# A fused attention, MLP and Strassen-gated MLP kernel: where the last layer's output products stand around the seventh product of a block of tokens

## The chip, the cores and the metric

The kernel runs on 1 core of a Trainium2 chip. The metric is the device time of one execution in microseconds (us); shorter is better. Engines are named as the profile names them: PE is TensorE's matmuls, PEld its weight loads, DVE is VectorE, ACT is ScalarE, POOL is GpSimd, SP is the queue that issues most of the DMAs.

## The reference

Three stages run one after the other on 3072 tokens. The change touches the last alone.

```
def reference(...):
    attn_out = _attn_ref(q, k, v, mem_k, mem_v)      # chunked attention, 4 x 8 heads x 768 x 64
    x = attn_out.transpose(0, 2, 1, 3).reshape(3072, 512)
    h = x @ w_in                                     # 512 -> 2048
    x = np.maximum(0.01 * h, h) @ w_out              # 2048 -> 512
    return ((x @ w_a) * (x @ w_b)) @ w2_out          # 512 -> 1536, gated, -> 512
```

All numbers are float32. The kernel splits each operand into a high and a low part (`hi`, `lo`), and takes three matmuls where a product of float32 numbers is wanted: low by high, high by low, high by high.

## The kernel before, in words

The last layer is computed for three blocks of 1024 tokens each (`sb` = 0, 1, 2; `NS` is 3), two halves of 512 tokens per block. Its 1536 hidden columns are taken in six pairs of 256 (`p` = 0..5; `k` counts all 18 pairs). Every 2 x 2 block product is done by Strassen's scheme in Winograd's form: seven products instead of eight.

`layer3(k, m)` is a generator that makes the seven products of one pair for `w_a` (`m` = 0) or `w_b` (`m` = 1). `stage(k, m, pos)` runs it on by one product, `pos` 0 to 6. A product is 6 matmuls 128x512 into one PSUM bank; the banks are called A, B, C and D, and A and C take more than one product each. At `pos` 4 VectorE adds the copied bank A (`u3`) to bank C (`done(1, 1, ...)`, L897); `pos` 5 is a product into D; `pos` 6, the seventh product, goes on accumulating into C and can do so only when that addition has read C. With `m` = 1 each sum is multiplied by what `m` = 0 left (`ga`) and is then split by `parts`: a cast on ACT (L126) and a subtraction on DVE (L127) make one `st` tile. `st` 0 comes after `pos` 1, `st` 2 after `pos` 4, `st` 1 after `pos` 5. After the seventh product `done(0, 1, ...)` adds the copied `u2` to C, and a chain of additions and subtractions on DVE makes four more: `st` 3, 4, 6 and 5, in this order.

`product4(sb, g, j, i)` is an output product: two pairs (a group `g`, three per block), row block `j` of 128 tokens (0 to 3), Strassen index `i` (0 to 6). It is 6 matmuls 128x256; the first three take the `st` tile of the even pair, the last three that of the odd pair, which is the newer one. Index 0, 4, 5 goes to a bank `oa`, the others to `oc`; there are two banks of each, so rows 2 and 3 take over those of rows 0 and 1. DVE adds banks to `acc` in SBUF (L982), and after the last group a row is stored.

Groups 0 and 1 of a block have their output products spread over the products of the next pair: `PLAN` says which batch of `BATCH` follows which `pos`. The last group of a block has no next pair of its own. There (`end`), PE is held to the order of the code (`pe.on`; the other engines are not, and a scheduler puts their instructions into an order when the program is built). For blocks 0 and 1 the batches are mixed with the first products of the next block: these are the two **changes of tokens**. For block 2 the list `LAST` is run: **the end**. At a change the operands of the next block, `xc_make(sb + 1, i)`, are made too: subtractions of 128x1024 on DVE (L754, `xs`), a cast on ACT (`ch`) and a subtraction on DVE (`cl`).

The lines 44 and 47 are those of `InOrder`, the helper that holds an engine to the order of the code: a matmul after `pe.on` has one of them, whatever it computes; the tiles tell it apart.

Of the kernel before, what the change touches and what calls it, by code (L numbers as in the profile page):

```python
# [53 lines left out]
def kernel(  # L54
# [680 lines left out]
    def xs_load(sb):  # L735
        for h, tag in enumerate(("xh", "xh" if sb else "xl")):
            t = xp.tile([P, KC, TB], F32, tag=tag, name="xs")
            nc.sync.dma_start(out=t, in_=x2d[2 * sb + h])
            xs[sb, h] = t
# [8 lines left out]
    def xc_make(sb, i):  # L748
        (b11, b21), (b12, b22) = [
            (xs[sb, h][:, 0:HC, :], xs[sb, h][:, HC:KC, :]) for h in range(2)  # L750
        ]

        def sub(out, x, y):
            nc.vector.tensor_tensor(out=out, in0=x, in1=y, op=ALU.subtract)  # L754

        if i == 0:
            xc_parts(sb, 0, b11)
            sub(b11, b12, b11)
        elif i == 1:
            xc_parts(sb, 1, b21)  # L760
        elif i == 4:
            xc_parts(sb, 3, b11)
            sub(b11, b22, b11)
            xc_parts(sb, 4, b11)
        elif i == 5:
            sub(b12, b22, b12)
            xc_parts(sb, 5, b12)
        elif i == 2:
            sub(b21, b21, b11)
            xc_parts(sb, 2, b21)  # L770
        elif i == 6:
            xc_parts(sb, 6, b22)
# [20 lines left out]
    for bi, f, parts in items[LEAD:]:  # L793
# [20 lines left out]
        if not first:  # L814
            wo_load((bi - 1) * NF1 + f + 4)

            i = (bi - 1) * NF1 + f
# [39 lines left out]
    def wt_load(sb, g, r):  # L857
        t = wq.tile([P, 2, 2, 256], F32R, tag="wt", name="wt", bufs=7)
        nc.sync.dma_start(out=t.bitcast(F32), in_=wtd[g][:, r])
        wts[sb, g, WT[r]] = t  # L860
# [92 lines left out]
    def product4(sb, g, j, i):  # L953
# [55 lines left out]
                store(1, low, both)  # L1009

    BATCH = (
# [6 lines left out]
    )  # L1018
    LAST = [(j, i) for j in range(4) for i in (0, 2)] + [(j, 3) for j in range(4)]
    LAST += [(j, i) for j in range(4) for i in (4, 6, 1, 5)]  # L1020

    def batch(sb, g, *ns):
        for n in ns:
            for j, i in BATCH[n]:
                product4(sb, g, j, i)
# [4 lines left out]
    def stage(k, m, pos):  # L1030
        if made.get((k, m), 0) == pos:
            next(stages[k, m])
            made[k, m] = pos + 1

    PLAN = (
        {2: (0, 1), 4: (2,), 5: (3,)},
        {0: (4,), 1: (5,)},
    )

    for k, (sb, p) in enumerate(pairs):  # L1040
        if p == 2 and sb + 1 < NS:
            xs_load(sb + 1)
        g, odd = divmod(p, 2)
        for m in range(2):
            end = p == NP - 1 and m == 1
            for pos in range(6):
                stage(k, m, pos)
                if pos == 0 and (k or m):
                    stage(*((k, 0) if m else (k - 1, 1)), 6)
                if not odd and p:  # L1050
                    batch(sb, g - 1, *PLAN[m].get(pos, ()))
                if odd and not m:
                    for r in (pos, 6)[:1 + (pos == 5)]:
                        wt_load(sb, g, r)
                if end and sb + 1 < NS and pos < 2:
                    xc_make(sb + 1, pos)
            if end:
                pe.on, pe.last = True, None
                stage(k, m, 6)
                if sb + 1 == NS:  # L1060
                    for j, i in LAST:
                        product4(sb, g, j, i)
                    break
                batch(sb, g, 0)
                stage(k + 1, 0, 0)
                batch(sb, g, 1)
                stage(k + 1, 0, 1)
                batch(sb, g, 2)
                xc_make(sb + 1, 4)
                batch(sb, g, 3)  # L1070
                xc_make(sb + 1, 5)
                batch(sb, g, 4)
                xc_make(sb + 1, 2)
                batch(sb, g, 5)
                xc_make(sb + 1, 6)
                for pos in range(2, 6):
                    stage(k + 1, 0, pos)
                pe.on = False
# [66 lines left out]
```

## Time and profile before

| | before |
|---|---|
| time, median of 3 runs | 1146.77 us (1145.92 to 1147.29) |
| the profiled execution's own time | 1145.8 us |
| its span, first to last instruction | 1144.0 us |
| PE busy | 1122.0 us, 98% |
| DVE busy | 803.2 us, 70% |
| ACT busy | 476.8 us, 42% |
| granted TensorE clock, mean | 0.996 of full speed |

Busy time is an average over three very different stages; what DVE does around the changed places is read from those places. Matmuls overlap, so that the distance from one start to the next tells what a matmul costs, and its own duration does not.

### The profile page before, as it was taken

What the parts mean: (1) busy time and instruction counts of PE and PEld (TensorE: products, weight loads), DVE (VectorE), ACT (ScalarE), POOL (GpSimd) and SP (SyncE); (2) the same over time, 40 slices, a digit from 0 to 9 for tenths busy, and PEclk for the clock granted to TensorE, in tenths of its full rate; (3) what the DMA queues carried; (4) which work ended last, traced back from release to release, by engine and by line L of the source; (5) the groups of instructions that cost most, each with busy time, mean ns of one, the idle gap of its engine ahead of it and who ended that gap; (6) DMA issues with size and microseconds to landing.
All of it is one profiled execution on the core that took longest, in us unless ns stands there. A gap on an engine that the chain in (4) does not pass through costs nothing.

```text
span 1144.0 us, 18008 instructions
## 1 busy us (share of the span) xinstructions
PE 1122.0 (98%) x6992; PEld 958.6 (84%) x6992; DVE 803.2 (70%) x1485; ACT 476.8 (42%) x806; POOL 6.3 (1%) x16
## 2 busy tenths in 40 slices
PE   6899999999999999999999999999999999999998
PEld 6678888888888888888888898989898979898987
DVE  6899499879978964645112838597747689656767
ACT  5787565555555544325223424152333142333221
POOL 2000000000000000000000000000000000000000
PEclk9999999999999999999999999999999999999999
DMA  9977899899999984326346765657856566747451
GB/s 349 328 267 283 313 327 312 319 349 336 308 345 331 333 312 166 124 93 225 106 147 224 254 211 176 203 165 259 277 172 204 173 207 212 231 155 227 148 184 74
DMA packets 89380, 269.68 MB, mean 236 GB/s; under 512 B 9552, under 2 KB 10960, under 8 KB 88528
## 3 DMA queue, kind: packets, MB, share of 16 engines
q1 hardware_dynamic: 88992, 268.21, 69.0%
q8 instruction: 55, 0.90, 0.3%
q10 hardware_dynamic: 304, 0.33, 0.1%
q14 instruction: 29, 0.24, 0.1%
HBM read 214.50 MB, written 54.00 MB: 235 GB/s over the span
## 4 chain that ended last, share of the span: by engine, by line
PE 86%; DVE 5%; DMA 2%; ACT 1%; issue 0%; SPq 0%; DVEq 0%; ACTq 0%
PE h L413 7%; PE a L533 7%; PE a L537 7%; PE a L536 7%; PE h L415 6%; PE h L414 6%; PE A L868 4%; PE A L869 4%; PE A L870 4%; PE C L868 3%; PE C L869 3%; PE C L870 3%; PE oc L972 2%; PE oc L971 2%; PE oc L970 2%; PE oc L47 2%
## 5 line engine op out<-in xcount | busy, mean ns | idle before, releaser
L413 PE MATMUL h<-xh,w 128*128 128x512 f32 (+1 forms) x384 | 151.8, 395 | 3.1 <-ACT w L47 3.1
L533 PE MATMUL a<-gh,w 128*128 128x512 f32 (+1 forms) x392 | 150.8, 385 | 0.9 <-DVE w L183 0.7
L536 PE MATMUL a<-gl,w 128*128 128x512 f32 (+1 forms) x392 | 150.5, 384 | 0.0
L537 PE MATMUL a<-gh,w 128*128 128x512 f32 (+1 forms) x392 | 150.4, 384 | 0.0
L415 PE MATMUL h<-xh,w 128*128 128x512 f32 (+1 forms) x384 | 149.2, 388 | 0.0
L414 PE MATMUL h<-xl,w 128*128 128x512 f32 (+1 forms) x384 | 149.0, 388 | 0.0
L431 DVE TENSOR_TENSOR gl<-g,gh 128x512 fp32r<-128x512 f32 (+1 forms) x96 | 65.2, 679 | 95.0 <-ACT gh L430 94.3
L126 ACT CAST st<-gb 128x512 fp32r<-128x512 f32 x126 | 76.5, 621 | 107.5 <-DVE gb L897 107.2
L515 ACT ACTIVATE g<-h 128x512 f32<-128x512 f32 (+1 forms) x96 | 56.3, 587 | 110.6 <-PE h L415 110.1
L127 DVE TENSOR_TENSOR st<-gb,st 128x512 fp32r<-128x512 f32 x126 | 85.3, 689 | 12.9 <-ACT st L126 10.7
L893 ACT COPY u<-A 128x512 f32<-128x512 f32 x72 | 42.2, 586 | 124.5 <-PE A L870 114.6
L413 PEld LDWEIGHTS h<-xh,w 128*128 128x128 f32 x384 | 72.4, 188 | 18.6 <-ACT w L47 3.2
L533 PEld LDWEIGHTS a<-gh,w 128*128 128x128 f32 x392 | 73.8, 188 | 16.3 <-DVE w L183 1.1
L536 PEld LDWEIGHTS a<-gl,w 128*128 128x128 f32 x392 | 73.8, 188 | 14.5
L537 PEld LDWEIGHTS a<-gh,w 128*128 128x128 f32 x392 | 73.7, 188 | 14.5
L415 PEld LDWEIGHTS h<-xh,w 128*128 128x128 f32 x384 | 72.4, 189 | 14.8
L414 PEld LDWEIGHTS h<-xl,w 128*128 128x128 f32 x384 | 72.5, 189 | 14.1 <-DVE xl L47 0.4
L346 DVE STREAM_TRANSPOSE pt<-p 32x128 f32<-32x128 f32 x256 | 77.4, 303 | 4.3
L868 PE MATMUL A<-ch,wab 128*128 128x512 f32 x204 | 79.5, 390 | 0.0
L869 PE MATMUL A<-cl,wab 128*128 128x512 f32 x204 | 79.5, 390 | 0.0
L870 PE MATMUL A<-ch,wab 128*128 128x512 f32 x204 | 79.4, 389 | 0.0
L897 DVE TENSOR_TENSOR ga<-u,C 128x512 f32<-128x512 f32 x36 | 24.7, 686 | 55.8 <-PE C L870 36.2
(162 smaller groups left out, 2331.6 us busy)
## 6 DMA issues: line engine op xcount, KB each, us to landing
wab<-wab SPq DMA_DIRECT2D x126, 512.0 KB, 4.3
w<-wod SPq DMA_DIRECT2D x80, 512.0 KB, 4.7
raw<-w SPq DMA_DIRECT2D x68, 512.0 KB, 6.7
wt<-wtd SPq DMA_DIRECT2D x63, 512.0 KB, 4.8
k<-kl SPq DMA_DIRECT2D x48, 256.0 KB, 4.8
v<-vl SPq DMA_DIRECT2D x48, 256.0 KB, 5.0
wab<-pwb SPq DMA_DIRECT2D x12, 768.0 KB, 6.3
wod<-w SPq DMA_DIRECT2D x16, 512.0 KB, 6.2
```

What stands on the lines that cost most here:

```text
L126: act.copy(hi, z)
L127: eng.tensor_tensor(out=lo, in0=z, in1=hi.bitcast(F32), op=ALU.subtract)
L346: dve.transpose(out=pt[o0:o0 + 32, :, 2 * cpar + hpar, hpx, :], in_=p[i0:i0 + 32, hpx::2, 32 * b:32 * b + 32],)
L413: pe.matmul(ps, w[1], x[0], start=first, stop=False)
L414: pe.matmul(ps, w[0], x[1], start=False, stop=False)
L415: pe.matmul(ps, w[0], x[0], start=False, stop=last)
L533: pe.matmul(ps, slot[:, 1, c], gh[:, t], start=f == 0 and o == 0, stop=False, **kw)
L536: pe.matmul(ps, slot[:, 0, c], gl[:, t], start=False, stop=False, **kw)
L537: pe.matmul(ps, slot[:, 0, c], gh[:, t], start=False, stop=f == NF1 - 1 or (o == HALF and f == LEAD - 1), **kw)
L868: pe.matmul(ps, w[:, 1, c], hi[:, kc], start=first and kc == 0, stop=False, **kw)
L869: pe.matmul(ps, w[:, 0, c], lo[:, kc], start=False, stop=False, **kw)
L870: pe.matmul(ps, w[:, 0, c], hi[:, kc], start=False, stop=kc == HC - 1, **kw)
```

## The change

At a change of tokens the first batch, rows 0 and 1 of index 0 and 2, is split in two: index 0 of both rows comes ahead of the seventh product, index 2 behind it. The products of index 3 come behind the second product of the next block instead of between its first and second. `PLAN` is renumbered for the longer list, so in the six groups inside the blocks the order of the same four products becomes 0, 0, 2, 2 instead of 0, 2, 0, 2. At the end the same two products of index 0 come ahead of the seventh product, and the products of index 3 of rows 2 and 3 move from the common start into rows 0 and 1.

```
     BATCH = (
-        [(0, 0), (0, 2), (1, 0), (1, 2)],
+        [(0, 0), (1, 0)],
+        [(0, 2), (1, 2)],
         [(0, 3), (1, 3)],
         [(0, 4), (0, 6), (0, 1), (1, 4), (1, 6), (1, 1)],
...
-    LAST = [(j, i) for j in range(4) for i in (0, 2)] + [(j, 3) for j in range(4)]
-    LAST += [(j, i) for j in range(4) for i in (4, 6, 1, 5)]
+    LAST = [(2, 0), (3, 0)] + [(j, 2) for j in range(4)] + [(0, 3), (1, 3)]
+    for j in range(4):
+        LAST += [(j, i) for i in (4, 6, 1)] + [(j + 2, 3)] * (j < 2) + [(j, 5)]
...
     PLAN = (
-        {2: (0, 1), 4: (2,), 5: (3,)},
-        {0: (4,), 1: (5,)},
+        {2: (0, 1, 2), 4: (3,), 5: (4,)},
+        {0: (5,), 1: (6,)},
     )
...
                 pe.on, pe.last = True, None
+                batch(sb, g, 0)
                 stage(k, m, 6)
...
-                batch(sb, g, 0)
+                batch(sb, g, 1)
                 stage(k + 1, 0, 0)
-                batch(sb, g, 1)
                 stage(k + 1, 0, 1)
-                batch(sb, g, 2)
+                batch(sb, g, 2, 3)
                 xc_make(sb + 1, 4)
-                batch(sb, g, 3)
+                batch(sb, g, 4)
                 xc_make(sb + 1, 5)
-                batch(sb, g, 4)
+                batch(sb, g, 5)
                 xc_make(sb + 1, 2)
-                batch(sb, g, 5)
+                batch(sb, g, 6)
                 xc_make(sb + 1, 6)
```

On PE, at the first change of tokens, the order differs as follows (`-` before, `+` changed). A row is an instruction: tile written, tiles read, shape. `C_7512` is the bank of the seventh product, `oa` the banks of index 0, `st_7495` the `st` 0 of the newer pair.

```order
-L44 MATMUL C_7512<-ch6_5926,wab_7430 128x512
+L44 MATMUL oa_7548<-wt_7398,st_7299 128x256
+L47 MATMUL oa_7548<-wt_7398,st_7299 128x256 x2
+L47 MATMUL oa_7548<-wt_7398,st_7495 128x256 x3
+L47 MATMUL oa_7556<-wt_7398,st_7299 128x256 x3
+L47 MATMUL oa_7556<-wt_7398,st_7495 128x256 x3
+L47 MATMUL C_7512<-ch6_5926,wab_7430 128x512
```

Two output products, 12 matmuls, now stand between the sixth product and the seventh.

On DVE, at the same place, the kernel before has this order from the addition that reads the finished C to the subtraction that makes `st` 3 (`st_7560`), and on to `st` 4 (`st_7565`).

```order
L897 TENSOR_TENSOR gb_7556<-u2_7510,C_7512 128x512
L127 TENSOR_TENSOR st_7532<-gb_7529,st_7532 128x512
L897 TENSOR_TENSOR gb_7556<-gb_7556,ga_7478 128x512
L127 TENSOR_TENSOR st_7545<-gb_7542,st_7545 128x512
L897 TENSOR_TENSOR gb_7529<-gb_7556,gb_7529 128x512
L982 TENSOR_TENSOR acc_6527<-acc_6527,oa_7575 128x256
L897 TENSOR_TENSOR gb_7556<-gb_7492,gb_7556 128x512
L127 TENSOR_TENSOR st_7560<-gb_7529,st_7560 128x512
L897 TENSOR_TENSOR gb_7492<-gb_7529,gb_7492 128x512
L982 TENSOR_TENSOR acc_6527<-acc_6527,oa_7590 128x256
L897 TENSOR_TENSOR gb_7542<-gb_7542,gb_7492 128x512
L127 TENSOR_TENSOR st_7565<-gb_7492,st_7565 128x512
```

The changed kernel has this order on DVE there (`st_7532` is `st` 2, `st_7576` is `st` 3, `st_7581` is `st` 4).

```order
L982 TENSOR_TENSOR acc_6527<-acc_6527,oa_7548 128x256
L127 TENSOR_TENSOR st_7532<-gb_7529,st_7532 128x512
L127 TENSOR_TENSOR st_7545<-gb_7542,st_7545 128x512
L982 TENSOR_TENSOR acc_6527<-acc_6527,oa_7556 128x256
L897 TENSOR_TENSOR gb_7572<-u2_7510,C_7512 128x512
L754 TENSOR_TENSOR xs_6461<-xs_6463,xs_6461 128x1024
L897 TENSOR_TENSOR gb_7572<-gb_7572,ga_7478 128x512
L754 TENSOR_TENSOR xs_6463<-xs_6463 128x1024
L897 TENSOR_TENSOR gb_7529<-gb_7572,gb_7529 128x512
L897 TENSOR_TENSOR ga_7623<-a1_7612,B_7614 128x512
L897 TENSOR_TENSOR gb_7572<-gb_7492,gb_7572 128x512
L127 TENSOR_TENSOR st_7576<-gb_7529,st_7576 128x512
```

The additions of index 0 and the tiles `st` 2 and `st` 1 moved ahead of the addition that reads C; two subtractions for the next block (L754) and the next block's `ga_7623` moved in between that addition and `st` 3. Behind the last row come, one after the other, `gb_7492`, the addition of index 3 of row 0, `gb_7542`, and `st` 4. The second change of tokens has the same orders with other numbers.

On PE, at the end, the changed kernel has this order behind the products of index 2 (`st_10861`, `st_10866`, `st_10870` are `st` 3, 4, 6 of the newest pair).

```order
L47 MATMUL oc_10892<-wt_10736,st_10861 128x256 x3
L47 MATMUL oc_10899<-wt_10736,st_10687 128x256 x3
L47 MATMUL oc_10899<-wt_10736,st_10861 128x256 x3
L47 MATMUL oa_10835<-wt_10748,st_10692 128x256 x3
L47 MATMUL oa_10835<-wt_10748,st_10866 128x256 x3
L47 MATMUL oc_10892<-wt_10725,st_10696 128x256 x3
L47 MATMUL oc_10892<-wt_10725,st_10870 128x256 x3
```

One product of index 3 (row 1) stands between that of row 0 and the first of index 4, where before three did.

## Rows read from the trace of the kernel before

**Rows 1.** The page, its first line.

```profile
span 1144.0 us, 18008 instructions
```

**Rows 2.** Who PE waited for, whole span: us in total, times, longest.

```profile
PE s L44 <- DMA k<-kl: 5.4, 1, 5.4
...
PE C L44 <- DVE gb L897: 1.8, 2, 0.9
...
PE oa L47 <- DVE acc L982: 0.9, 1, 0.9
...
PE oc L47 <- DVE st L127: 0.6, 2, 0.3
```

**Rows 3.** Timeline of PE, first change: start, us, instructions, [idle before <-releaser].

```profile
762.36 0.39 PE L870 MATMUL D<-ch,wab 128*128 128x512 f32 x1
763.67 0.50 PE L44 MATMUL C<-ch,wab 128*128 128x512 f32 x1 [0.92 <-DVE gb L897]
764.01 0.40 PE L47 MATMUL C<-cl,wab 128*128 128x512 f32 x1
...
766.73 0.62 PE L47 MATMUL oc<-wt,st 128*128 128x256 f32 x3 [0.31 <-DVE st L127]
...
770.01 1.60 PE L47 MATMUL oc<-wt,st 128*128 128x256 f32 x12
771.45 0.40 PE L47 MATMUL B<-ch,wab 128*128 128x512 f32 x1
...
777.14 1.60 PE L47 MATMUL oa<-wt,st 128*128 128x256 f32 x12
...
780.02 2.01 PE L47 MATMUL oa<-wt,st 128*128 128x256 f32 x12
```

**Rows 4.** Busy time in the first change of tokens: PE, PEld, DVE, ACT, POOL, clock, DMA.

```profile
756.00:791.00 35.00, 33.62 (x225) 30.60 (x224) 34.54 (x51) 12.27 (x18) 0.00 (x0) 1.00 0.56 174
```

**Rows 5.** Timeline of DVE, first change.

```profile
762.33 0.69 DVE L127 TENSOR_TENSOR st<-gb,st 128x512 fp32r<-128x512 f32 x1
762.93 0.68 DVE L897 TENSOR_TENSOR gb<-u,C 128x512 f32<-128x512 f32 x1
...
764.13 1.29 DVE L897 TENSOR_TENSOR gb<-gb,ga 128x512 f32<-128x512 f32 x2
...
768.39 0.41 DVE L982 TENSOR_TENSOR acc<-acc,oa 128x256 f32<-128x256 f32 x1
768.73 0.68 DVE L897 TENSOR_TENSOR gb<-gb 128x512 f32<-128x512 f32 x1
769.33 0.68 DVE L127 TENSOR_TENSOR st<-gb,st 128x512 fp32r<-128x512 f32 x1
...
776.84 1.22 DVE L754 TENSOR_TENSOR xs<-xs 128x1024 f32<-128x1024 f32 x1
777.98 0.68 DVE L982 TENSOR_TENSOR acc<-acc,oc 128x512 f32<-128x512 f32 x1
```

**Rows 6.** Timeline of PEld, first change: the weight load of the seventh product.

```profile
763.67 0.19 PEld L44 LDWEIGHTS C<-ch,wab 128*128 128x128 f32 x1 [1.35 <-DVE gb L897]
```

**Rows 7.** Timeline of PE, the end.

```profile
1116.73 0.39 PE L870 MATMUL D<-ch,wab 128*128 128x512 f32 x1
1117.21 0.50 PE L44 MATMUL C<-ch,wab 128*128 128x512 f32 x1
...
1130.58 1.70 PE L47 MATMUL oa<-wt,st 128*128 128x256 f32 x12 [0.93 <-DVE acc L982]
...
1139.32 0.88 PE L47 MATMUL oa<-wt,st 128*128 128x256 f32 x6
```

**Rows 8.** Busy time and clock, microseconds 23 and 26, columns as in rows 4.

```profile
23.00:24.00 1.00, 1.00 (x10) 0.77 (x9) 0.97 (x2) 0.69 (x5) 0.00 (x0) 0.50 1.05 426
...
26.00:27.00 1.00, 1.00 (x9) 1.00 (x8) 0.97 (x3) 0.61 (x2) 0.00 (x0) 0.82 1.03 410
```

**Rows 9.** Timeline of PE ahead of those microseconds.

```profile
21.18 0.38 PE L47 MATMUL h<-xh,w 128*128 128x256 f32 x1 [1.34 <-ACT xh L47]
```

## The prediction

> **What bounds the kernel now.** The list of what PE waited for comes first [rows 2]: apart from waits at the very start (the longest is 5.4 us, for the first keys), the waits that the change can touch are four lines long. The seventh product waits for the addition that reads C twice, 0.9 us each; an index 2 product waits for its `st` tile twice, 0.3 us; one product at the end waits 0.9 us for a bank. No DMA stands in these places, so the moved stores and loads on the SP queue are costed at nothing: what covers them is that PE's late waits are all for DVE.
>
> The timeline of PE shows what such a wait costs [rows 3]. 512-column matmuls start 0.23 us apart, so D's last slot ends at 762.59; C starts at 763.67, which is 1.08 us lost, and its second matmul comes 0.34 us later instead of 0.23: 0.11 us more for starting again. Twelve 256-column matmuls take 771.45 - 770.01 = 1.44 us, 0.12 each and 0.72 a product. The index 2 wait shows 0.31 us idle.
>
> The busy time of the same stretch is the view that decides [rows 4]: in 35 us around the first change DVE is busy 34.5 us, PE 33.6. DVE is as full there as PE. The kernel's 70% for DVE hides this. So the question is not whether the C wait goes, but in which order DVE does the same work.
>
> **The change, part by part.** Inside the blocks four products change their order in six groups; the `st` tiles are old there, and DVE's order stays the same, so 0. If a tile were late after all it would show as a wait of the kind in [rows 2]; there is none outside the listed places.
>
> *The first change of tokens*, walked with these steps: on DVE [rows 5] a 512-wide instruction 0.60 us after the one before (762.33, 762.93), 256-wide 0.34 (768.39, 768.73), 1024-wide 1.14 (776.84, 777.98), results 0.08 us later; handing over takes 0.06 (an `st` 0 that starts at 762.33 and lasts 0.69 is free to PE at 763.08).
>
> PE: index 0 of rows 0 and 1 starts at 762.59, waits 0.11 us for `st` 0 at 763.08 in the middle, ends at 764.25. C follows with no wait, since its reader ends at 763.61: the 1.08 us are gone. C ends at 765.6; the second half of index 2 would start at 765.98.
>
> DVE: the two multiplications at 764.13 and 764.73, then by the new order the addition of index 0 at 765.33, `st` 2 at 765.66, done 766.34. PE waits until 766.40, 0.43 us, as before. Index 2 ends at 767.58, the next block's A at 768.95, B at 770.31; the first half of index 3 at 770.67. Now it needs `st` 3.
>
> DVE's list up to `st` 3: `st` 1 at 766.26, an addition at 766.86, the reader of C at 767.19, the first subtraction for the next block at 767.79, a multiplication at 768.93, the second subtraction at 769.53, the sum at 770.67, `ga` of the next block at 771.27, a difference at 771.87, `st` 3 at 772.47 to 773.15. Before, the same tile was made at 769.33 [rows 5] and PE had reached index 3 at 770.01 [rows 3], with 0.3 us to spare for its second half. Now PE waits from 770.67 to 773.21: **2.54 us**, and three instructions of 1.14, 1.14 and 0.60 us are the reason. ACT adds nothing: its casts for the next block end before the `st` 3 cast is wanted at DVE.
>
> Then the rest of the chain is late too, since nothing stands between index 3 and index 4 any more, where before the 1.4 us of B stood. DVE: difference 773.07, index 3's addition at 773.83 (it needs the product), difference 774.43, `st` 4 at 775.03 to 775.71. PE has done (1, 3) at 774.4 and half of (0, 4) at 774.75: a wait of 1.02 us. `st` 6 follows an addition at 775.63 and is free at 776.97; PE waits 0.38 us. With 0.1 us for each new start, four more products bring PE to index 5 at 780.3. Before that was 777.14 [rows 3]: +3.17 us. One hidden wait goes (the twelve matmuls at 780.02 last 2.01 us instead of 1.60, so 0.41), and one like it comes, 0.31 us, for the addition of index 3 of row 2. **+3.1 us a change**, +6.2 for two, since the waits at the second change are the same to 0.1 us [rows 2]. Bounds: 2.5 us, the one large wait without its followers minus the removed C wait and so +1.3, if DVE catches up at once; 4.1, if every hand-over costs 0.1 more. All of it lies on the path, for PE has no slack behind it.
>
> *The end* is walked with the same steps, from D's last slot at 1116.96 [rows 7]. The start of C loses 0.25 + 0.11 us now, and the bank wait 1.08 + 0.1; both go: -1.5. The seventh product ends at 1119.77, 1.07 us later than before (1.44 of index 0 less 0.36), and only two rather than four products of index 3 stand ahead of index 4. The addition at `pos` 4 starts at 1116.47 (its end released C at 1117.21), and by its list DVE reads the finished C at 1120.3 and makes `st` 3 seven instructions later: free at 1124.7 where PE wants it at 1124.45. Five more make `st` 4 free at 1127.3 against 1126.2, and `st` 6 is 0.38 us late. With new starts that is +1.9. Sum: +0.3 us, PE ending at 1140.4 instead of 1139.32 + 0.72 = 1140.04. The last additions and stores behind it are the same. Bounds: -1.5, if the tiles are in time, and +1.5.
>
> [...]
>
> **TensorE's clock.** [...] I take it that the clock falls at each change of tokens for about 3.3 us (23 to 26, and 0.18 / 0.5 of the next). Half of that, 1.65 us, is the upper bound; but part of this time PE waits for DVE anyway, which a slower PE waits less for, so I charge 0.35 us each, +0.7. Below: 0.
>
> **Sum.** 6.2 + 0.3 + 0.7 = +7.2 us on the profiled execution's 1145.8 us (span 1144.0 [rows 1], 1.8 around it): 1153.0. The median of the runs shown is 0.97 above that execution, so 1154.0.
>
> **Rivals.**
> (a) Faster: the waits of [rows 2] go and nothing takes their place, -1.2 a change and -1.5 at the end, 1142.9 us. It decides at `st` 3: if DVE has it by 770.6, 2.5 us ahead of my walk, there is no wait. For it: DVE did so before, with the two next-block subtractions at 776.84 and later. Against it: the order of the built program has them ahead, DVE runs its instructions in that order in every row, and it has only half a microsecond of idle time in 35 to catch up with.
> (b) Nothing moves: a wait merely changes places. With DVE's old order the reader of the finished C (765.8) stands ahead of `st` 2 (766.4 to 767.1), and PE waits 1.1 us at index 2 instead of 1.08 at C: +0.1 a change, +0.3 at the end, 1147.3 us. It would need a DVE order other than that of the built program.
> (c) Slower than I say: the clock falls at each change and, because of the waits for `st` 4 and `st` 6, stays down for a second stretch: 1.65 more each, 1157.3 us. For it: 1.4 us of waits fall into the first stretch. Against: at 26 us it came back.
> (d) The late tiles cost less, because what runs between two DVE rows is shorter than my steps: at the lower bound, +1.3 a change, no clock loss: 1149.7.
>
> **How the numbers follow.** Forecast 0.66, (a) 0.05, (b) 0.07, (c) 0.12, (d) 0.10. A measurement of this kernel can tell some 0.2%, 2.3 us. Faster by more: (a), 0.05. Within: (b) and a small part of (d), 0.08. Slower: 0.87. The forecast with its bounds spans 1151 to 1156; a range from 1150.3 to 1156.8 takes in the better part of (d) and some of (c), and leaves out under 2 in 10.
>
> **What would show it.** PE's waits: the line of C gone or near 0; a line of `oc` for the `st` subtraction with its longest at 2.5 us, twice; `oa` for the same subtraction with 1 us, three times; index 2 still 0.3 us. On DVE two `xs` subtractions within 4 us of the addition that reads the finished C. PE's start of the next block's third product (A again, behind index 5 of rows 2 and 3) 3 us later, counted from D. The clock below 1 in one or two microseconds after the wait. Wrong would be: a `st` 3 that lands within 6 us of C's end, or a clock that falls for longer than one stretch.

## The result, and the profile after

The changed kernel took 1153.15 us (median of 5 runs, 1152.04 to 1154.05), the kernel before 1146.77 (1145.25 to 1147.29, 5 runs): ratio 1.006, 95% interval 1.0048 to 1.0071, that is 5.5 to 8.1 us slower. The forecast was 1154.0, between 1150.3 and 1156.8. The profiled execution of the changed kernel is the slowest of its five (1154.05). One execution of the kernel `end` of experiment 1 took 2259.22 us, for a reason not known, and is left out of its ratio.

The page's first line after, beside the 1144.0 us of [rows 1]:

```profile
span 1152.3 us, 18002 instructions
```

The list of what PE waited for, in the columns of [rows 2]:

```profile
PE s L44 <- DMA k<-kl: 6.4, 1, 6.4
PE oc L47 <- DVE st L127: 5.7, 6, 2.4
...
PE oa L47 <- DVE st L127: 0.9, 1, 0.9
```

The seventh product's line (C, 1.8 us) is gone, and so is the bank wait at the end (0.9). In their place PE waits 5.7 us for `st` tiles in products into `oc` (index 2, 3 and 6), where it was 0.6, and 0.9 us at the end in one into `oa` (index 4). The first line, the wait for the first keys, is the kernel's start-up, ahead of anything that changed.

PE's timeline at the first change of tokens, to be read against [rows 3]:

```profile
763.13 0.39 PE L870 MATMUL D<-ch,wab 128*128 128x512 f32 x1
763.36 0.28 PE L44 MATMUL oa<-wt,st 128*128 128x256 f32 x1
...
765.02 0.40 PE L47 MATMUL C<-ch,wab 128*128 128x512 f32 x1
...
767.18 1.34 PE L47 MATMUL oc<-wt,st 128*128 128x256 f32 x9 [0.26 <-DVE st L127]
...
771.10 0.51 PE L47 MATMUL oc<-wt,st 128*128 128x256 f32 x3
773.99 2.29 PE L47 MATMUL oc<-wt,st 128*128 128x256 f32 x9 [2.37 <-DVE st L127]
776.07 1.57 PE L47 MATMUL oa<-wt,st 128*128 128x256 f32 x6
...
778.18 1.33 PE L47 MATMUL oc<-wt,st 128*128 128x256 f32 x9 [0.18 <-DVE st L127]
...
793.38 0.40 PE L47 MATMUL A<-ch,wab 128*128 128x512 f32 x1
```

The first half of an index 3 product (three matmuls, 0.12 us each from start to start) fills PE's time to 771.10 + 0.36 = 771.46, and the next start is at 773.99: 2.53 us lost. What a change of tokens costs is measured from the start of D's last matmul to the start of the next block's third product (the last row): 793.38 - 763.13 = 30.25 us. Before, it was 26.71, from D at 762.36 to this row of the kernel before:

```profile
789.07 0.40 PE L47 MATMUL A<-ch,wab 128*128 128x512 f32 x1
```

That is +3.54; at the second change 26.69 became 30.25, +3.56. This stretch is the measure in all that follows.

DVE's timeline there, against [rows 5]:

```profile
767.98 0.68 DVE L897 TENSOR_TENSOR gb<-u,C 128x512 f32<-128x512 f32 x1
768.57 1.22 DVE L754 TENSOR_TENSOR xs<-xs 128x1024 f32<-128x1024 f32 x1
...
770.31 1.22 DVE L754 TENSOR_TENSOR xs<-xs 128x1024 f32<-128x1024 f32 x1
...
772.05 0.68 DVE L897 TENSOR_TENSOR ga<-a,B 128x512 f32<-128x512 f32 x1
...
773.25 0.68 DVE L127 TENSOR_TENSOR st<-gb,st 128x512 fp32r<-128x512 f32 x1
```

Between the addition that reads the finished C (767.98) and `st` 3 (773.25) stand the two subtractions for the next block and its `ga`.

The clock in single microseconds, columns as in [rows 4]:

```profile
772.00:773.00 1.00, 0.00 (x0) 0.00 (x0) 1.00 (x3) 1.00 (x2) 0.00 (x0) 1.00 0.65 70
773.00:774.00 1.00, 0.01 (x1) 0.01 (x1) 1.00 (x3) 0.13 (x1) 0.00 (x0) 0.84 1.00 410
774.00:775.00 1.00, 1.00 (x4) 1.00 (x5) 0.53 (x1) 0.43 (x1) 0.00 (x0) 0.50 0.12 45
...
777.00:778.00 1.00, 0.99 (x6) 0.79 (x6) 1.00 (x2) 0.49 (x1) 0.00 (x0) 0.96 0.00 0
```

The mean of 0.84 in microsecond 773 means that the clock fell near 773.7, while PE stood still (to 773.99). It stays at 0.50 to about 777.1 (0.96 in microsecond 777): some 3.4 us, of which PE had work in 3.1. The matmuls behind the wait show it: nine take 2.29 us, where the nine at 767.18 take 1.34.

PE's timeline at the end, against [rows 7]:

```profile
1124.59 0.39 PE L870 MATMUL D<-ch,wab 128*128 128x512 f32 x1
...
1135.14 0.63 PE L47 MATMUL oa<-wt,st 128*128 128x256 f32 x3 [0.91 <-DVE st L127]
...
1136.34 2.06 PE L47 MATMUL oc<-wt,st 128*128 128x256 f32 x15 [0.22 <-DVE st L127]
...
1147.60 0.88 PE L47 MATMUL oa<-wt,st 128*128 128x256 f32 x6
```

From D's last matmul to the last product 23.01 us, before 1139.32 - 1116.73 = 22.59: +0.42. The three places add up to 3.54 + 3.56 + 0.42 = 7.5 us in this execution; another 0.77 of the span lies ahead of the first change (762.36 against 763.13), and all of it already ahead of the last layer, whose first matmul starts at 609.19 before and at 609.96 after.

### The profile page after: what moved, and what is told of

Same layout as the page of the kernel before. It is cut to its first block, busy times and chain, and to the rows that moved or that the text cites. A ratio compares the mean times of both kernels' runs of the same rounds, so it can differ in the third digit from the quotient of the medians.

```text
span 1152.3 us, 18002 instructions
## 1 busy us (share of the span) xinstructions
PE 1126.8 (98%) x6992; PEld 963.0 (84%) x6992; DVE 803.6 (70%) x1485; ACT 476.4 (41%) x806; POOL 6.3 (1%) x16
## 4 chain that ended last, share of the span: by engine, by line
PE 89%; DVE 5%; issue 0%; ACT 0%; DVEq 0%; ACTq 0%
PE h L413 7%; PE a L533 7%; PE a L537 7%; PE a L536 7%; PE h L415 7%; PE h L414 7%; PE A L868 4%; PE A L869 4%; PE A L870 4%; PE C L868 3%; PE C L869 3%; PE C L870 3%; PE oc L47 2%; PE oc L972 2%; PE oc L970 2%; PE oc L971 2%
```

## The experiments

The order theory: at the changes of tokens DVE is full, and what counts is what stands on DVE ahead of `st` 3; PE's waits follow from it. Its rivals are the cover theory (only PE's own order counts, and a wait that has work in its place is gone) and the load theory (DVE has too much work there, in whatever order). For the clock the rivals are that its fall costs all that half the clock could cost, or nothing.

### 1. The parts by themselves: end, plan

The kernel before with the new end alone, and with the order 0, 0, 2, 2 inside the blocks alone (a seventh batch, used by `PLAN`):

```
+    LAST = [(2, 0), (3, 0)] + [(j, 2) for j in range(4)] + [(0, 3), (1, 3)]
...
+                if sb + 1 == NS:
+                    product4(sb, g, 0, 0)
+                    product4(sb, g, 1, 0)
                 stage(k, m, 6)
```

```
+        [(0, 0), (1, 0), (0, 2), (1, 2)],
...
-        {2: (0, 1), 4: (2,), 5: (3,)},
+        {2: (6, 1), 4: (2,), 5: (3,)},
```

Expected of the end:

> The kernel before with the new order of the end alone (two products of index 0 ahead of the last seventh product, and the rows taken one by one). Order theory, by the profiles: the wait at C and the bank wait go, waits of 1 us for st 4 and 0.2 to 0.4 for st 3 and st 6 come; +0.4 us from the last D to the last matmul (23.0 against 22.6), not to be told from no change in the time. If the end carried the loss: 6 us.

Expected of the order inside the blocks:

> The kernel before with the new order of the four products inside the blocks alone (0, 0, 2, 2 in the six groups), changes of tokens and end as before. All theories of the changes: 0 us, no new PE wait. If the order inside the blocks carried part of the loss, up to 1 us a group, 6 us.

Measured: the end 1146.33 us, ratio 1.0002 (0.9993 to 1.0011), its stretch (D's last matmul to the last product) 1140.39 - 1117.39 = 23.00 us, +0.41; the order inside the blocks 1146.06 us, ratio 0.9999 (0.999 to 1.0007). Neither can be told from no change. The loss is at the two changes of tokens.

### 2. DVE's order held: hold

The changed kernel, PE's order as it is, but the next block's subtractions and its first `ga` may be issued on DVE only behind `st` 5 (the operands of index 3 stay early):

```
+        chain[i] = w_parts(w[:, 0, :], w[:, 1, :], t, nc.vector).ins
...
+            with tc.issue_after(chain[5]) if sb and i > 1 else ExitStack():
+                nc.vector.tensor_tensor(out=out, in0=x, in1=y, op=ALU.subtract)
```

> The changed kernel, with one thing held on VectorE: at a change of tokens the subtractions for the next block, the parts made of them and the next block's first sum may be issued only behind the subtraction that makes st 5. PE's order is that of the change. Order theory (the added time comes from three VectorE instructions that the new order puts ahead of st 3): the 2.4 us waits at the second half of index 3 shrink to about 0.2 us, twice; the waits for st 4 and st 6 (1.0 and 0.4) stay, one bank wait of about 0.8 us for the late additions comes; the clock does not fall. From D to the next block's third product 28.1 us a change, against 30.25 in the changed kernel and 26.7 before; in all 4.3 us less than the changed kernel, about 3 us above the kernel before. Cover theory (the new PE order leaves index 4 without products ahead of it, whatever VectorE does first): no change against the changed kernel, 6 to 8 us above the kernel before.

Measured: 1148.84 us, ratio 1.0024 (1.0016 to 1.0033); the stretch 28.29 and 28.30 us. PE's timeline of it:

```profile
770.44 1.33 PE L47 MATMUL oc<-wt,st 128*128 128x256 f32 x9 [0.21 <-DVE st L128]
771.61 0.52 PE L47 MATMUL oa<-wt,st 128*128 128x256 f32 x3
773.05 0.62 PE L47 MATMUL oa<-wt,st 128*128 128x256 f32 x3 [0.92 <-DVE st L128]
...
781.31 1.70 PE L47 MATMUL oa<-wt,st 128*128 128x256 f32 x12 [0.69 <-DVE acc L989]
```

The wait for `st` 3 falls from 2.37 us to 0.21 with PE's order untouched, and the mean clock of the execution is 0.999. So DVE's order made the large wait; DVE's work is the same in both kernels, so a load theory without order can't explain it. But the stretch is still 1.6 us above before, with waits for `st` 4 (0.92), `st` 6 (0.22) and the accumulators (0.69). Holding the order takes away 1.95 of the 3.55, and some 0.37 of this is the clock, which stays up here too (experiment 5).

### 3. Where those 1.6 us come from: between, hold_between

Index 3 back between the next block's first and second product, once in the changed kernel and once in the held one:

```
                 stage(k + 1, 0, 0)
+                batch(sb, g, 2)
                 stage(k + 1, 0, 1)
-                batch(sb, g, 2, 3)
+                batch(sb, g, 3)
```

> The changed kernel with the products of index 3 put back between the next block's first and second product, so that B's 1.4 us stand ahead of index 4 again as they did before. VectorE's built order now has the two subtractions for the next block and two of their low parts (1.14 us each) ahead of st 3 and st 4. Order theory: the wait at index 3 grows to about 3.9 us, index 4 still waits 1.2, index 6 0.4: 4.7 us a change more than before without the clock, some 10 us in all: slower than the changed kernel by about 3 us. Cover theory: with the cover back the waits for st 4 and st 6 go, 1.4 us a change less than the changed kernel: about 3 us faster than it.

> The changed kernel with DVE's order held, and index 3 back between the next block's first and second product, as in the kernel before; with the order held, the stretch was 28.3 us, 1.6 more than before, and this run asks where that comes from. Theory (DVE's chain is late: the additions of index 0 and st 1 now stand ahead of the addition that reads C, and st 3 comes 8.5 us after D in place of 7.5): moving the second product only moves the wait, 1.5 us for st 3 and hardly any for st 4, in place of 0.2 and 0.9; stretch 28.3 us again, by the walk to the hundredth. Rival (the second product's 1.4 us were the cover that is missing ahead of st 4): the wait for st 4 goes and nothing takes its place, 27.0 to 27.2 us, time some 2.4 us below the held version.

Measured: the first 1155.07 us, ratio 1.0076 (1.0064 to 1.0088), stretch 30.97 and 30.98, +4.27 on before. The walk had 4.7 without the clock, and the clock fell here too, so it was 0.4 too long or more; the wait of 1.2 us that it had at index 4 does not show, as B's matmuls ran at a clock of 0.52 and 0.50 there (microseconds 775 and 776). Its `st` 3 waits are 3.66 and 3.68 us, and three 1.14 us instructions for the next block stand between the reader of C and `st` 3 on DVE. The second kernel took 1149.61 us, ratio 1.0033 (1.0021 to 1.0044), stretch 28.28 and 28.30, as expected. Its PE timeline:

```profile
770.24 1.33 PE L47 MATMUL oc<-wt,st 128*128 128x256 f32 x9 [1.57 <-DVE st L128]
...
789.83 0.40 PE L47 MATMUL A<-ch,wab 128*128 128x512 f32 x1
```

With the second product behind index 3 the wait for `st` 3 is 1.57 and the one for `st` 4 disappears; the sum is the same to a hundredth. The place of the second product moves the wait and doesn't make it. What is late is DVE's chain: in the held kernel the second half of index 3 gets `st` 3 at 770.44, 8.46 us behind D's last slot (761.98); in the kernel before it is free at 770.07, 7.48 behind 762.59. DVE in the held kernel, from the reader of C to `st` 3:

```profile
766.59 0.68 DVE L903 TENSOR_TENSOR gb<-u,C 128x512 f32<-128x512 f32 x1
767.31 0.69 DVE L903 TENSOR_TENSOR gb<-gb,ga 128x512 f32<-128x512 f32 x1
768.03 1.42 DVE L903 TENSOR_TENSOR gb<-gb 128x512 f32<-128x512 f32 x2
769.70 0.69 DVE L128 TENSOR_TENSOR st<-gb,st 128x512 fp32r<-128x512 f32 x1 [0.25 <-ACT st L126]
```

The reader of C in the kernel before:

```profile
765.38 0.69 DVE L897 TENSOR_TENSOR gb<-u,C 128x512 f32<-128x512 f32 x1
```

With two index 0 products ahead of the seventh, DVE does their additions, `st` 2 and `st` 1 before it reads C, 4.61 us behind D's last slot in place of 2.79. But `st` 2, `st` 1 and one addition stood ahead of `st` 3 before as well, between the steps of the chain. New ahead of it is one addition, 0.34 us. The other 0.65 of the late microsecond is that the chain's steps, with nothing between them, come further apart. A step that reads what the one before wrote starts 0.72 us after it here (766.59, 767.31, 768.03) in place of 0.60, and `st` 3 waits another 0.25 for its cast on ACT, so that the four steps take 3.11 us in place of 4 x 0.60. And 0.55 of the 1.6 us is not the chain: the wait for the accumulators (781.31) costs 0.96 us with its restart, where the hidden wait of the kernel before (780.02 in [rows 3]) cost 0.41. No run tried whether a DVE order with other work between these steps gives some of this back.

### 4. A smaller dose: one

The kernel before with one product, index 0 of row 0, ahead of the seventh at the two changes:

```
+                if sb + 1 < NS:
+                    product4(sb, g, 0, 0)
                 stage(k, m, 6)
...
-                batch(sb, g, 0)
+                for j, i in BATCH[0][1:]:
+                    product4(sb, g, j, i)
```

> The kernel before with a single output product, index 0 of row 0, ahead of the seventh product at the two changes of tokens, and nothing else changed; a smaller dose that covers 0.7 of the 1.08 us that the seventh product waits. DVE's order in the built program has one subtraction for the next block (1.14 us) ahead of st 3 and the next block's ga between st 4 and st 6. Order theory, walked with the steps of the prediction: the seventh product waits 0.1, index 2 waits 0.9 in place of 0.3, st 3 and st 4 0.85 each; stretch 28.7 us in place of 26.7, time 4 us above the kernel before. Cover theory (a wait that is covered is gone): 26.0 us, time 1.4 us below.

Measured: 1149.69 us, ratio 1.0039 (1.0024 to 1.0053); the stretch 28.82 and 28.84 us, 0.1 above the walk that DVE's built order gave. PE's timeline:

```profile
765.75 0.62 PE L47 MATMUL oc<-wt,st 128*128 128x256 f32 x3 [0.73 <-DVE st L127]
...
770.33 1.33 PE L47 MATMUL oc<-wt,st 128*128 128x256 f32 x9 [0.78 <-DVE st L127]
...
774.13 0.62 PE L47 MATMUL oa<-wt,st 128*128 128x256 f32 x3 [0.73 <-DVE st L127]
```

Three waits of 0.7 to 0.8 us stand where before there was one of 0.92 and one of 0.31. The cover theory forecast 26.0 us and falls.

### 5. The price of the clock: fill

The changed kernel with 18 extra matmuls (results unused) in the wait for `st` 3:

```
                 stage(k + 1, 0, 1)
+                for _ in range(18):
+                    pe.matmul(oc[1][:, 1], st[sb, 2 * g, 3][:, 0, 0:P],
+                              wts[sb, g, 3][:, 0, 0], start=True, stop=True, ...)
                 batch(sb, g, 2, 3)
```

> The changed kernel, and behind the second product of the next block, where PE waits 2.4 us for st 3, 18 matmuls 128x256 whose result is never used (into a bank that index 3 overwrites right after); 18 x 0.12 = 2.16 us, so they end before st 3 is there and PE hardly stops. Theory (the clock falls because PE stands still, and that costs about 0.4 us a change on top of the waits): the granted clock stays at 1.00 through both changes, the waits for st 4 (about 1.0 us) and st 6 (0.4) become visible, since PE's work no longer stretches over them, and the stretch from D's last matmul to the next block's third product is 29.9 us in place of 30.25; time 0.8 us below the changed kernel's. Rival 1, the half clock costs all that it could, 3.2 x 0.5 = 1.6 us a change: 28.7 us, time 3.2 us lower. Rival 2, it costs nothing, since DVE is late anyway: 30.25 us, same time. Rival 3, the clock falls whatever PE does there: it is at 0.50 again and the stretch is no shorter.

Measured: 1152.38 us, ratio 1.0054 (1.0042 to 1.0067). The changed kernel's interval overlaps this one, so the stretch decides: 29.88 and 29.86 us. Its busy time and clock, and PE's timeline:

```profile
770.00:774.00 4.00, 3.90 (x28) 3.46 (x26) 4.00 (x7) 3.10 (x4) 0.00 (x0) 1.00 0.34 104
774.00:778.00 4.00, 2.75 (x19) 2.35 (x19) 3.89 (x8) 1.76 (x3) 0.00 (x0) 1.00 0.09 31
```

```profile
774.11 1.34 PE L47 MATMUL oc<-wt,st 128*128 128x256 f32 x9 [0.21 <-DVE st L127]
...
776.72 0.62 PE L47 MATMUL oa<-wt,st 128*128 128x256 f32 x3 [0.92 <-DVE st L127]
```

The clock stays at 1.00 and the stretch is 0.37 to 0.39 us shorter. The second half of index 3 starts 10.86 us behind D's last matmul in both kernels, so the filling moved nothing else. The waits for `st` 4 and `st` 6 are there now; in the changed kernel PE's slow matmuls stretched over them. Half the clock over the 3.1 us in which PE had work could take some 1.6 us; three quarters of that fell into time in which PE would have waited anyway.

### 6. Less work for DVE: pool_after, pool_hold_after, pool_hold_before

Three of the next block's subtractions per change on GpSimd (indices 4, 5 and 2), in the changed kernel, in the held one, and in the kernel before with the hold. In the last two the subtractions themselves are no longer held, while the next block's low parts (`cl`) on DVE are, those of index 3 too. The edit of the last two; the first names the three indices instead:

```
+            eng = nc.gpsimd if sb and i > 1 else nc.vector
+            eng.tensor_tensor(out=out, in0=x, in1=y, op=ALU.subtract)
```

> The changed kernel with three of the next block's subtractions 128x1024 per change (indices 4, 5 and 2) on GpSimd in place of VectorE: 3 x 1.14 us less work for DVE at each change. In the order of the built program one subtraction of 1.14 us and the next block's ga still stand ahead of st 3, where two subtractions and ga did. Order theory (what counts is what stands between the reader of C and st 3): the wait for st 3 shrinks by 1.14 us to about 1.2, the stretch from D to the third product from 30.25 to 28.7 to 29.1 us, time 1150.2 to 1151. Load theory (DVE is simply full, and every microsecond taken off it comes back): 3.4 us less, 26.8 us, the time of the kernel before. Third possibility, GpSimd and VectorE slow each other down: the DVE rows beside GpSimd's are longer than 0.68 and 1.22 us, and the stretch stays at 30 or more.

> The changed kernel with DVE's order held (the next block's subtractions and its first ga only behind st 5) and the three subtractions on GpSimd. Order theory: with the order held the three subtractions no longer stood ahead of any st tile, so only the wait for the accumulators (0.7 us, index 0 of rows 2 and 3) goes: stretch 27.6 us in place of 28.3, time about 1147.5, still not below the kernel before, since the waits for st 4 and st 6 (0.9 and 0.2) come from PE's own order. Load theory: 3.4 us less again, 24.9 us, 1142. If GpSimd takes so long that the next block's operands are late, or slows DVE: over 28.3.

> The kernel before with the same held order and the three subtractions on GpSimd; a candidate for beating both. Order theory: the seventh product's wait shrinks from 1.08 us to about 0.5 (a subtraction of 1.14 us no longer stands ahead of st 0) and the hidden wait of 0.41 us for the accumulators goes; index 2 waits a little longer: stretch 26.0 to 26.5 us in place of 26.7, time 0.4 to 1.4 us below the kernel before, 1145.4 to 1146.4. Load theory: 3.4 us less a change, 24.5 us (what PE needs without any wait), 1142.4. If GpSimd is slow or slows DVE: above 26.7.

Measured: 1166.44 us, ratio 1.0184 (1.0165 to 1.0204), stretch 36.64 and 36.66; 1161.08, 1.0127 (1.0111 to 1.0142), 34.72 and 34.08; 1155.2, 1.0079 (1.0065 to 1.0092), 31.47 and 31.15. All three are slower than what they were made from: the third possibility of each expectation came, and the walks of the order theory were 5 to 8 us too short, as they had no term for it. The timelines of GpSimd and DVE in the first:

```profile
764.49 5.55 POOL L755 TENSOR_TENSOR xs<-xs 128x1024 f32<-128x1024 f32 x2 [2.29 <-DVE cl L127]
```

```profile
764.94 0.67 DVE L898 TENSOR_TENSOR gb<-u,C 128x512 f32<-128x512 f32 x1
765.54 0.68 DVE L898 TENSOR_TENSOR gb<-u,D 128x512 f32<-128x512 f32 x1
766.14 4.46 DVE L898 TENSOR_TENSOR gb<-gb,ga 128x512 f32<-128x512 f32 x2
```

Two subtractions take GpSimd 5.55 us, and two multiplications on DVE beside them, which take 1.29 us alone [rows 5], take 4.46, to just behind GpSimd's end (770.04). The clock falls in this stretch too: C's first matmuls start 0.42 us apart (766.69, 767.11) in place of 0.23, and the mean clock of the execution is 0.993. So these runs didn't relieve DVE: they don't test what less work on DVE would be worth, and show only why this way of taking it off doesn't pay here.

None of the ten kernels beats the kernel before; the closest are the end and the order inside the blocks alone, which are the same as before.

## Why the prediction was right, step by step

**What bounds the place.** Right: DVE's order. With it held, PE's idle time of 2.37 us ahead of `st` 3 is 0.21 (hold).

**The seventh product's wait** is gone, and index 0 loses 763.36 to 765.02 less 1.44, 0.22 us, in place of 0.11. **Index 2** loses 0.41 (766.41 + 0.36 to 767.18; forecast 0.43).

**`st` 3**: forecast 2.54, measured 2.53, from the three instructions that the prediction named.

**`st` 4 and `st` 6**: forecast 1.02 and 0.38 beside 0.1 for each new start. In the changed kernel they are hardly visible, because the clock had fallen; with the clock kept up, `st` 4 costs 775.65 to 776.72, 1.07, and `st` 6 0.38 (777.18 + 0.36 to 777.92). The forecast profile "1 us, three times" was therefore wrong for two of the three places (only the end has it), while the sum was right: without the clock's fall a change costs 29.88 - 26.71 = 3.17, forecast 3.1.

**The reason given for these waits** was half right. "Nothing stands between index 3 and index 4 any more" says where PE waits; hold_between shows that, with DVE's order held, the second product back in that place changes nothing in the sum. What remains is that the chain on DVE is late: by one more addition, and by steps that come further apart.

**The clock**: forecast 0.35 a change, measured 0.37 to 0.39. This is in part luck. The prediction gives bounds of 0 and 1.65 and no working for 0.35. No run shows that term, which was the author's estimate; fill showed 0.37 to 0.39 in its place. The fall early in the kernel before is weak ground for it: 1.34 us of idle time [rows 9] went with a fall [rows 8], 1.57 in hold_between did not. The length was right (3.4 us at 0.50, forecast 3.3), though its sign, one or two microseconds below 1, was not. Rival (c), that the clock stays down for a second stretch, didn't come: it is at 0.96 in microsecond 777.

**The end**: forecast +0.3 (its own times, 1140.4 less 1140.04, make it 0.36), measured +0.41 by itself. **Inside the blocks**: 0, measured ratio 0.9999.

**The sum**: 7.2 forecast, 7.5 in the three stretches of the profiled execution, 6.4 between the medians. The mean clock of the profiled execution is 0.994, and 0.996 to 0.997 in the three fastest of the five. They have no trace, so whether the clock fell in them at both changes is open. The agreement to 0.3 us is one of the profiled execution; the medians agree to 0.8.

**The rivals**: (a), nothing takes the waits' place, fell with the first `st` 3 row. (b), waits only change places, fell as a forecast of this kernel. What it needed, DVE's old order with the reader of C ahead of `st` 2, no run has: in the held kernel `st` 2, `st` 1 and both additions still stand ahead of that reader, and the stretch grows by 1.6 us. So what PE's new order would cost under the old DVE order is not shown. (d) needed a shorter `st` 3 wait than the 2.53 us measured.

The new start's 0.1 us is in the held kernel's rows: three matmuls take 0.52 us in the stream (771.61) and 0.62 behind a wait (773.05), as [rows 3, 6] had it.

## What to carry to other kernels

Before filling a wait on one engine with other work, ask whether the engine that it waits for has time to spare at that place. Take the busy share from the stretch itself, not from the page. On a full engine early work for one consumer is late work for the next. The built order of that engine, walked with durations from rows, gave the price here within 0.2 us a stretch for the change itself and for hold, hold_between, one and fill (these four were walked when the changed kernel's trace was known). It was 0.4 us or more off in between, and 5 to 8 us off in the three kernels with subtractions on GpSimd: beside these, instructions on DVE took 4.46 us in place of 1.29 (pool_after) and 3.44 in place of 1.22 (pool_hold_before), for which the walk had no term. A fall of the clock behind a wait cost little here (0.37 us of a possible 1.6), since PE would soon have waited again.

## What the runs showed of the hardware that was not expected

**Beside a GpSimd subtraction, DVE was late here where both operands were in SBUF, and not where one was in PSUM.** During the 5.55 us of GpSimd's two subtractions in pool_after, DVE's additions with one operand in PSUM ran at their usual 0.67 and 0.68. The two multiplications with both operands in SBUF took 4.46 us in place of 1.29 and ended at 770.60, 0.56 us behind the second subtraction's end (770.04). The kernel before with the subtractions on GpSimd (pool_hold_before) shows one subtraction beside one DVE instruction with both operands in SBUF:

```profile
761.13 2.60 POOL L759 TENSOR_TENSOR xs<-xs 128x1024 f32<-128x1024 f32 x1 [753.88 <-DVE xs L759]
```

```profile
761.38 3.44 DVE L128 TENSOR_TENSOR cl<-xs,ch 128x1024 fp32r<-128x1024 f32 x1
```

761.13 + 2.60 = 763.73, and 1.1 us later the DVE instruction ends; alone it lasts 1.22. What holds the DVE instructions back, these rows do not show. The subtraction itself took GpSimd 2.6 to 2.9 us in these three kernels, beside DVE's work, against 1.22 on DVE.

**The clock did not always fall during the wait.** In the kernel "between" it was still at 1.00 through a wait of 3.66 us and fell 1.5 us after PE had started again:

```profile
773.53 1.33 PE L47 MATMUL oc<-wt,st 128*128 128x256 f32 x9 [3.66 <-DVE st L127]
```

```profile
774.00:775.00 1.00, 1.00 (x10) 0.96 (x9) 1.00 (x2) 0.00 (x0) 0.00 (x0) 1.00 0.00 0
775.00:776.00 1.00, 1.00 (x4) 0.81 (x3) 1.00 (x3) 0.15 (x1) 0.00 (x0) 0.52 0.00 0
```

Then it stayed at 0.50 through microsecond 777. In the changed kernel, behind 2.37 us, it fell some 0.3 us before the wait was over (near 773.7, with PE's next start at 773.99). A wait of 1.57 us in hold_between left it at 1.00:

```profile
765.00:770.00 5.00, 3.40 (x21) 2.74 (x20) 4.66 (x8) 2.31 (x4) 0.00 (x0) 1.00 0.37 105
770.00:771.00 1.00, 0.77 (x6) 0.77 (x7) 0.89 (x3) 0.19 (x1) 0.00 (x0) 1.00 0.00 0
```

What decides when it falls was not tried.
